# TensorE's turning of the first product's values ends after 12 jobs instead of 16 in the second MoE of a fused kernel

## The chip, the cores and the metric

The kernel runs on one core of a Trainium2 chip as one program. The core has five engines that run side by side, each its own list of instructions in order: TensorE (PE; the loading of its stationary operand is listed apart as PEld), VectorE (DVE), ScalarE (ACT), GpSimd (POOL) and SyncE (SP, which here only issues DMA transfers). An instruction waits on semaphores for what it needs, and everything behind it on the same engine waits with it. The metric is the device time of one execution in microseconds; the median of three runs is given, and the profile is one further execution of the same program.

## What is computed

Three parts follow one another: a chunked scan with decay ("attention"), a feed-forward layer h * cos(h) on its output, and a mixture of experts with one expert a token, 8 experts and a capacity. The change lies in the third part:

```python
def _moe2_ref(x, w_gate, w1, w2, capacity):      # x: 3072 x 256, w1: 8 x 256 x 1024, w2: 8 x 1024 x 256
    logits = x @ w_gate
    expert_idx = np.argmax(logits, axis=1)
    ...                                          # disp: each expert's tokens, in order, up to capacity
    h = np.maximum(np.einsum('ecd,edf->ecf', disp, w1), 0.0)
    y = np.einsum('ecf,efd->ecd', h, w2)
    out = np.zeros((N, D), dtype=np.float32)
    for i in range(N):
        if keep[i]:
            out[i] = gate_w[i] * y[expert_idx[i], pos[i]]
    return out.astype(np.float32)
```

## The kernel before, in words

**Blocks and jobs.** The tokens are sorted by expert into blocks of 128 tokens; each block belongs to one expert. 29 blocks are always computed. A job is a block and one half of the inner dimension (512 of 1024). Jobs 0 to 15 are the first halves of blocks 0 to 15; then come blocks 16 to 28 with both halves one after the other (job 16 is block 16's first half, job 17 its second, 18 and 19 are block 17's, 20 and 21 block 18's, and so on); last come the second halves of blocks 0 to 15. While the first 16 jobs run, other engines still prepare the weights of the second half (`w1b`, `w2b`), from transfers on SP at L1223.

**The steps of a job**, in the names of the code. `b_gather` (POOL, L1535) fetches a block's rows into `xr`, and `b_xt` (SP, L1552) turns them by a transposing transfer into `xk` (blocks 0 to 15 keep theirs in `xkeep`, since it serves two jobs far apart). `b_mm1` (TensorE, L1603) makes the first product in 6 matmuls into `hp`, in PSUM. `b_relu` (ScalarE, L1609) writes its positive part as f16 into the first half of `hr`; `b_low` (VectorE, L1613) writes what f16 has rounded off into the second half. Then `hr` (128 tokens by 2 x 512 values) has to be turned into `ht`, eight blocks of 128 x 128, so that the inner dimension lies on partitions. There are two ways for that in `b_turn`: for jobs below `NPT`, TensorE does eight transposes into PSUM (`tp`, L1630) and `b_tev` copies them to `ht` on ScalarE (L1639); for all others one transposing transfer on SP's queue writes `ht` from `hr` (L1634). `b_mm2` (TensorE, L1650) makes the second product in 12 matmuls into `yp`; `b_out` scales it by `sc` and writes or adds it to `yacc` (ScalarE at L1662 for first halves, VectorE at L1664 for second halves); `b_scat` (POOL, L1669) writes a finished block's rows to the output.

**Buffers.** `hr` takes a buffer of tag `g`, which has 6; `ht` takes one of the same 6, save for every fourth job, whose `ht` takes one of the 3 of tag `gl`, which the `xk` of blocks 16 and on use too. So a new `hr` or `ht` waits until the last reader of the old tile in its buffer is done: a turn on TensorE or a transfer on SP for an `hr`, the second product for an `ht`.

**What sets the order.** Every step is put on a list with a number from the table `PLACE`, by its kind and count (`'b1'` first product, `'br'` ReLU, `'bl'` low part, `'bt'` turn and, for jobs below `NPT`, its copy, `'b2'` second product, `'bx'` the transfer of `xk`, and so on). The list is sorted by these numbers, and each engine gets its instructions in that order. Before, the turns of jobs 12 to 15 have the places 1697, 1720, 1725 and 1749, their copies 1721, 1727, 1739 and 1754, and their second products 1740, 1744, 1760 and 1772.

## Time and profile before

| | us |
|---|---|
| three runs | 573.99, 568.50, 570.76 |
| median | 570.76 |
| the profiled execution, its own time | 568.56 |
| its span in the profile | 566.8 |

| busy, us (share of the span) | |
|---|---|
| TensorE, matmuls | 528.7 (93%) |
| VectorE | 415.7 (73%) |
| ScalarE | 379.2 (67%) |
| GpSimd | 355.6 (63%) |

Times in the trace count from the start of the span. The profile is read at four depths: the page's head and its busy shares; the busy time of each engine in a stretch, with the granted clock of TensorE and the busy share of the DMA engines; the chain of waits, followed back from the last instruction to what released each step; and single instructions in order of time, SP's queue among them. Arrows point from what is read to what is written: `ht<-hr` writes `ht` from `hr`.

## The change

`NPT` becomes 12, so jobs 12 to 15 take the second way of `b_turn`, the transposing transfer on SP; their copies by `b_tev` go, and with them their four numbers in the list `'bt'`. The four places 1697, 1720, 1725 and 1749, at which TensorE turned, are now those at which SP issues the transfers. No other number changes. The table is one line shorter, so each line of the changed kernel's code has a number that is lower by one (L1634 is L1633 there).

```diff
     'bt': [1533, 1534, 1562, 1593, 1587, 1588, 1594, 1596, 1605, 1617, 1622, 1628, 1636, 1644,
-        1653, 1655, 1661, 1671, 1674, 1688, 1685, 1690, 1705, 1713, 1697, 1721, 1720, 1727,
-        1725, 1739, 1749, 1754, 1765, 1763, 1779, 1780, 1794, 1800, 1821, 1813, 1826, 1844,
...
+        1653, 1655, 1661, 1671, 1674, 1688, 1685, 1690, 1705, 1713, 1697, 1720, 1725, 1749,
+        1765, 1763, 1779, 1780, 1794, 1800, 1821, 1813, 1826, 1844, 1845, 1851, 1865, 1880,
...
-    NPT = MSPL
+    NPT = 12
```

SP's queue before, from the last weight transfers ahead of job 12's turn to the first transfers of `ht`. `xk_4826`, `xk_4909`, `xk_4964` and `xk_5065` are those of blocks 16, 17, 18 and 19, `xkeep2_4548` is block 15's; `ht_5023` is job 17's, `ht_5027` job 16's. In brackets stand the semaphores that an issue waits for: DMAHW and DMASW are landings of earlier transfers, by slot.

```order
L1223 DMA wst3_4681<-in_w2_dram 128x4x256 [waits DMAHW5_49,DVE_49]
L1552 DMA_TRANSPOSE xk_4826<-xr_4577 128x4x128 [waits DMASW7_49,PE_49]
L1552 DMA_TRANSPOSE xkeep2_4548<-xr_4757 128x4x128 [waits DMAHW6_49,DMASW0_49]
L1223 DMA wst3_4843<-in_w2_dram 128x4x256 [waits DMAHW7_49,DMAHW0_49,DVE_49]
L1223 DMA wst2_4844<-in_w2_dram 128x4x256 [waits DMAHW1_49,DVE_49]
L1552 DMA_TRANSPOSE xk_4909<-xr_4831 128x4x128 [waits DMASW1_49,PE_49]
L1552 DMA_TRANSPOSE xk_4964<-xr_4895 128x4x128 [waits DMASW2_49,DMAHW2_49,PE_49,Activation_49]
L1634 DMA_TRANSPOSE ht_5023<-hr_4916 128x8x128 [waits DMAHW3_49,DVE_49,PE_49]
L1634 DMA_TRANSPOSE ht_5027<-hr_4942 128x8x128 [waits DMAHW5_49,DMAHW4_49,DVE_49]
L1552 DMA_TRANSPOSE xk_5065<-xr_4902 128x4x128 [waits DMAHW1_49,DMASW3_49,PE_49]
```

The same queue now, first from the same weight transfer to the two issues ahead of block 17's `xk`. `ht_4779`, `ht_4847` and `ht_4870` are those of jobs 12, 13 and 14; `xk_4819` and `xk_4884` are those of blocks 16 and 17.

```order
L1222 DMA wst3_4681<-in_w2_dram 128x4x256 [waits DMAHW5_49,DVE_49]
L1633 DMA_TRANSPOSE ht_4779<-hr_4721 128x8x128 [waits DVE_49]
L1551 DMA_TRANSPOSE xk_4819<-xr_4577 128x4x128 [waits DMAHW6_49,DMASW7_49,PE_49]
L1551 DMA_TRANSPOSE xkeep2_4548<-xr_4757 128x4x128 [waits DMAHW7_49,DMASW0_49]
L1222 DMA wst3_4836<-in_w2_dram 128x4x256 [waits DMAHW0_49,DVE_49]
L1222 DMA wst2_4837<-in_w2_dram 128x4x256 [waits DMAHW1_49,DVE_49]
L1633 DMA_TRANSPOSE ht_4847<-hr_4797 128x8x128 [waits DMAHW2_49,DVE_49,PE_49]
L1633 DMA_TRANSPOSE ht_4870<-hr_4822 128x8x128 [waits DMAHW3_49,DVE_49,PE_49]
L1551 DMA_TRANSPOSE xk_4884<-xr_4824 128x4x128 [waits DMAHW4_49,DMASW1_49]
```

Job 12's transfer stands behind the weight transfer, ahead of block 16's `xk`; those of jobs 13 and 14 stand behind the last two weight transfers and ahead of block 17's `xk`.

The second piece of SP's order follows right behind it. `xk_4937` is block 18's and `xk_5029` block 19's; `ht_4940` is job 15's, `ht_4987` job 17's and `ht_4991` job 16's.

```order
L1551 DMA_TRANSPOSE xk_4937<-xr_4872 128x4x128 [waits DMAHW5_49,DMASW2_49,PE_49]
L1633 DMA_TRANSPOSE ht_4940<-hr_4887 128x8x128 [waits DMAHW6_49,DVE_49]
L1633 DMA_TRANSPOSE ht_4987<-hr_4891 128x8x128 [waits DMAHW7_49,DMAHW6_49,DVE_49]
L1633 DMA_TRANSPOSE ht_4991<-hr_4915 128x8x128 [waits DMAHW0_49,DVE_49]
L1551 DMA_TRANSPOSE xk_5029<-xr_4877 128x4x128 [waits DMAHW1_49,DMAHW4_49,DMASW3_49,PE_49]
```

Job 15's transfer stands between block 18's `xk` and job 17's transfer. Job 17's `ht_4987` lies in the buffer of `hr_4887`, from which job 15's transfer reads, and waits for that transfer's landing (slot DMAHW6); before, job 17's stood right behind block 18's `xk` and waited for a turn of TensorE instead.

ScalarE before, from job 14's ReLU (`hr_4829`) to job 15's (`hr_4912`). `ht_4833`, `ht_4863` and `ht_4897` are the copies for jobs 11, 12 and 13.

```order
L1609 ACTIVATE hr_4829<-hp2_4725 128x512
L1639 ACTIVATE ht_4833<-tp_4809 128x1024
L1662 ACTIVATE yacc1_4762<-yp2_4788,sc_4777 128x256
L1639 ACTIVATE ht_4863<-tp_4779 128x1024
L1639 ACTIVATE ht_4897<-tp_4854 128x1024
L1662 ACTIVATE yacc1_4762<-yp2_4873,sc_4835 128x256
L1231 ACTIVATE w2b_4579,wsc4_4842<-wst3_4843 128x4x256
L1231 ACTIVATE w2b_4579,wsc4_4842<-wst2_4844 128x4x256
L1609 ACTIVATE hr_4912<-hp2_4866 128x512
```

And now, from job 14's ReLU (`hr_4822`) to job 15's (`hr_4887`); `ht_4826` is job 11's copy.

```order
L1608 ACTIVATE hr_4822<-hp2_4725 128x512
L1638 ACTIVATE ht_4826<-tp_4802 128x1024
L1661 ACTIVATE yacc1_4762<-yp2_4781,sc_4777 128x256
L1661 ACTIVATE yacc1_4762<-yp2_4857,sc_4828 128x256
L1230 ACTIVATE w2b_4579,wsc4_4835<-wst3_4836 128x4x256
L1230 ACTIVATE w2b_4579,wsc4_4835<-wst2_4837 128x4x256
L1608 ACTIVATE hr_4887<-hp2_4850 128x512
```

Two copies are gone from between the outputs of jobs 10 and 11; the outputs' order and job 15's ReLU behind them stay.

## Rows read from the trace of the kernel before

**Rows 1.** The page's head.

```profile
span 566.8 us, 10500 instructions
```

**Rows 2.** Busy time of the engines by stretch; the first line names the columns.

```profile
core 0: us, PE busy (x) PEld busy (x) DVE busy (x) ACT busy (x) POOL busy (x), PEclk, DMA share, GB/s
416.40:418.60 2.20, 0.06 (x1) 0.00 (x0) 2.20 (x4) 2.08 (x4) 0.00 (x0) 1.00 0.50 75
418.60:421.20 2.60, 2.54 (x7) 0.86 (x7) 0.69 (x3) 0.94 (x3) 1.38 (x3) 0.52 0.41 89
...
445.00:455.00 10.00, 10.00 (x68) 6.49 (x67) 7.50 (x15) 4.52 (x8) 2.91 (x7) 1.00 0.95 148
```

**Rows 3.** The same view, TensorE alone: its busy time, clock, DMA share.

```profile
435.50:438.50 3.00, 3.00 (x25) 1.00 0.97 275
438.50:443.00 4.50, 4.50 (x42) 1.00 0.28 67
```

**Rows 4.** The chain of waits, 425 to 460: start, duration in us, what.

```profile
432.56 0.45 PE tp L1630 x8
...
436.25 0.45 PE tp L1630 x8
...
439.31 0.45 PE tp L1630 x8
...
442.36 1.31 PE yp L1650 x12
...
443.79 0.47 PE tp L1630 x8
...
450.74 2.62 PE yp L1650 x24
```

**Rows 5.** SP's queue in order of time: start, duration in us, transfer, count.

```profile
432.60 1.84 SPq L1223 DMA_DIRECT2D wst<-in_w_dram  x2
...
442.97 1.19 SPq L1552 DMA_TRANSPOSE xk<-xr  x1
...
445.05 2.62 SPq L1634 DMA_TRANSPOSE ht<-hr  x2
...
449.75 1.23 SPq L1634 DMA_TRANSPOSE ht<-hr  x1
```

**Rows 6.** Order of time, 428 to 456; in brackets the idle time and its releaser.

```profile
428.71 0.69 DVE L1613 SCALAR_TENSOR_TENSOR hr<-hp,hr 128x512 f16<-128x512 f32 x1
...
433.97 0.68 DVE L1613 SCALAR_TENSOR_TENSOR hr<-hp,hr 128x512 f16<-128x512 f32 x1
...
439.24 1.04 POOL L1535 DMA_INDIRECT xr<-xs_d,gat  x1 [0.16 <-POOL gall L1553]
439.40 0.47 ACT L1662 ACTIVATE yacc<-yp,sc 128x256 f32<-128x256 f32 x1 [1.33 <-PE yp L1650]
...
442.47 0.69 DVE L1613 SCALAR_TENSOR_TENSOR hr<-hp,hr 128x512 f16<-128x512 f32 x1 [3.47 <-ACT hr L1609]
...
448.37 0.60 ACT L1609 ACTIVATE hr<-hp 128x512 f16<-128x512 f32 x1 [1.09 <-DMA ht<-hr]
...
450.58 2.78 PE L1650 MATMUL yp<-w2a,ht 128*128 x24
...
454.15 1.08 ACT L1609 ACTIVATE hr<-hp 128x512 f16<-128x512 f32 x2 [0.27 <-DMA ht<-hr]
```

**Rows 7.** Groups by line: count, busy us, mean ns, idle before and releaser.

```profile
L1639 ACT ACTIVATE ht<-tp 128x1024 f16<-128x1024 f16 x16 | 16.1, 1029 | 1.0 <-PE tp L1630 0.9
```

**Rows 8.** The chain of waits, 495 to 520: a transfer on it.

```profile
509.67 3.21 DMA ht<-hr
```

**Rows 9.** Order of time, 505 to 520.

```profile
512.98 0.60 ACT L1609 ACTIVATE hr<-hp 128x512 f16<-128x512 f32 x1 [6.43 <-DMA ht<-hr]
...
513.99 1.89 PE L1650 MATMUL yp<-w2b,ht 128*128 x12 [1.63 <-ACT yacc L1662]
```

**Rows 10.** Order of time, 550 to 566: the last scatter but one.

```profile
558.92 0.97 POOL L1669 DMA_INDIRECT out_dram<-yacc,scat  x1 [1.73 <-DVE yacc L1664]
```

## What is expected of the change, and why

> **What bounds the kernel now.** I read the profile from the outside in. The page's head gives the span of the profiled execution, 566.8 us [rows 1]; its own time is 568.56, so 1.76 lie around the span. The three runs are 568.50, 570.76 and 573.99: the profiled execution lies 2.20 below their median, so I make the sum against 568.56 and carry the difference over to 570.76.

> Next, busy time by stretch. Jobs 12 to 15 are computed between 432.4 and 455.0, and there TensorE is busy 3.00 of 3.00 us, 4.50 of 4.50 [rows 3] and 10.00 of 10.00 [rows 2], all at a granted clock of 1.00, while in the last of these no other engine is full. The reader should also see the DMA share: 0.97 from 435.5 to 438.5, 0.28 from 438.5 to 443.0 [rows 3], 0.95 from 445.0 to 455.0 [rows 2]. Third, the chain of waits: from 432.56 to 450.74 + 2.62 = 453.36 it consists of TensorE alone, with the four turns that the change takes away among its pieces [rows 4]. So in this stretch whatever leaves TensorE moves everything behind it up, until something else is late. What that could be is read from the transfer queue on SP [rows 5] and from the neighbours in order of time [rows 6].

> **What is removed.** On TensorE, four turns of eight transposes: 0.45, 0.45, 0.45 and 0.47 us for jobs 12 to 15 [rows 4], together 1.82, all on the path. That is the most that can be gained; the least is nothing, where TensorE then waits for something that was not late before. On ScalarE, four copies out of PSUM at 1029 ns [rows 7], 4.1 us. They are not on the path: at 439.40 ScalarE has waited 1.33 us for a product of TensorE [rows 6], and the ReLUs of jobs 15 and 17 stand behind that wait. I cost their loss at nothing; those ReLUs can come up only with TensorE, by the two turns that stand ahead of that wait, 0.90 (432.56 and 436.25 [rows 4]).

> **What is added.** Four transposing transfers on SP, 2.62 us for two issues [rows 5], so 1.3 each and 5.2 in all. From issue to use a transfer took 3.21 us where the chain of waits went through one [rows 8]; 3.3 for the nearest one (issued 445.05 [rows 5], ScalarE released 448.37 [rows 6]); and 4.40 for the slowest near here (issued 449.75 [rows 5], ScalarE released 454.15 [rows 6]). It cannot land before its issue ends, so 1.3 is the lower bound. I take 3.21: two of the three rows lie there, and job 15's transfer will have as little around it.

> Job 12: its low part is done at 428.71 + 0.69 = 429.40 [rows 6], its product stands right behind the turn of 439.31 [rows 4], so at 439.76, less at most three turns, 1.35: not before 438.4. That leaves 9 us for a transfer of 3.21. Cost nothing; SP's queue behind it is put back by at most one issue, 1.3.

> Jobs 13 and 14: job 13's low part ends at 433.97 + 0.68 = 434.65 [rows 6] and job 14's is the next on VectorE, behind the two weight loads issued at 432.60 [rows 5]. Those keep the DMA engines busy until 438.5 [rows 3]; two transfers more bring me to 438.5 + 2 x 1.3 = 441.1, in a stretch where the share was 0.28. Job 13's lands at about 439.8; its product is the one of 442.36 [rows 4], which, less three turns, 1.35, comes to 441.0, so it is there in time. Job 14's product stands behind two first products more. Cost nothing; without that cover up to 1.3, which the next step would hide.

> Job 15 is the step that decides. Its low part ends at 442.47 + 0.69 = 443.16 [rows 6] before and some 0.8 earlier after the change, but its transfer stands on SP behind the xk of block 18 (jobs 20 and 21), which leaves SP at 442.97 + 1.19 = 444.16 [rows 5]. That xk waits for the gather issued at 439.24 [rows 6], which moves up by the one turn that stands ahead of what releases it, 0.45. So job 15's transfer is issued at 443.7 and has landed at 443.7 + 3.21 = 446.9. The next transfer, job 17's, now waits for that landing, because it is written into the buffer that job 15's values are read from (the second piece of SP's order in the section on the change). Before, it started at 445.05 [rows 5]; now at 446.9. Behind it on SP stands job 16's: issued at 448.2, landed at 451.4. TensorE wants it for the second of the two products of the row at 450.58 [rows 6], at 450.58 + 1.31 = 451.89 before (1.31 is one product in [rows 4]), and 1.82 earlier, at 450.07, after the change. It waits 1.3 us and starts at 451.4, 0.5 earlier than before. What stands behind on SP catches up: the next transfer but one is issued at 450.7 where it was issued at 449.75, lands at 453.9, and releases the ReLU that started at 454.15. So of 1.82 gained, 1.3 is given back. After the one wait of this size that the trace has, 1.63, twelve matmuls took 1.89 us [rows 9], where 24 in one run took 2.78 [rows 6], 1.39 for twelve: 0.5 lost. I take off 0.2, less than half of it, as the wait here is shorter. **Sum: 1.82 - 1.3 - 0.2 = 0.3 us gained.**

> From job 18 on the order and the waits on SP are those of before, one place for one; TensorE is busy there all the time but for that one wait, and the last scatter but one still waits 1.73 us for VectorE's sum behind TensorE's last products [rows 10]. So I let the 0.3 go through to the end.

> [...] Here eight blocks of 128 x 128 cost TensorE 0.45 us on its path [rows 4] and a transfer of eight blocks 3.21 us until it can be used [rows 8]. [...]

> **The rivals.** All three follow from the same sum with another latency L from issue to landing: job 16's transfer lands at 443.7 + 1.3 + 2L. (B) All 1.82 stay: it lands by 450.07, which needs L of 2.53 or less. For it: TensorE has no other wait here, and 2.53 lies above the bound of 1.3. Against it: all three latencies above. 570.76 - 1.82 = 568.94. (C) Slower, by the same queue: it lands after 451.89, from L = 3.45 on. At 4.40 job 15's lands at 448.1, job 16's is issued at 449.4 and lands at 453.8, 1.9 behind the product of before. [...] For it: the DMA share of 0.95 right there; against it: one latency of three is over 3.45. (D) The end is paced elsewhere and the change moves nothing, 570.76: at 512.98 ScalarE had waited 6.43 us for a transfer, and TensorE for ScalarE [rows 9]. Against it: that run of transfers is itself started by TensorE's products.

> **How the numbers follow.** My forecast (a gain from 0 to 1.0, likeliest 0.3) has 0.45; B 0.20; C 0.20; D 0.15. Likeliest for the profiled execution 568.56 - 0.3 = 568.3, for the median 570.76 - 0.3 = 570.5. The range runs from the lowest run with all gained, 568.50 - 1.82 = 566.7, to C, 574.0, which is also the highest run with nothing gained. 1% is 5.7 us, about what a measurement of this kernel can tell from no change. No case reaches it; runs of one kernel lie 5.5 apart, so I leave 0.03 for faster and 0.05 for slower.

> **What would show it.** Right: the turns on TensorE and ScalarE's copies fall from 16 to 12, transfers of ht rise from 42 to 46; on SP a gap of about 2 us between the transfers of jobs 15 and 17; TensorE idle for about a microsecond before a product near 450, released by the DMA of ht; its products after 455 about 0.3 earlier than before. Wrong: no wait of TensorE between 445 and 455 (B), a wait over 2 us or a granted clock below 1.00 after it (C), or a new wait ahead of 445, for jobs 13 or 14 or for the xk behind them.

## The result, and the profile after

The change makes the kernel slower: 574.40 us (median of 7 runs, 572.75 to 577.07) against 570.60 for the kernel before (7 runs on the same chip), a ratio of 1.0067 with a 95% interval of 1.0041 to 1.0093. Forecast were 570.5 and a small gain; the time lies just above the range, which ended at 574.0. It is within 1%, which had 0.92, but it is a loss of 3.8 us where the sum said 0.3 gained.

The page of the changed kernel: head and busy times, then ScalarE's copies among the groups by line. Its profiled execution took 577.07 us, the longest of the 7; that of before took 568.56, next to its shortest. So the two spans differ by 8.5 us where the medians differ by 3.8, and the amounts read from the two traces below are larger than the median's loss.

```profile
span 575.3 us, 10438 instructions
PE 529.9 (92%) x3156; PEld 385.9 (67%) x3156; DVE 416.2 (72%) x877; ACT 375.7 (65%) x687; POOL 357.4 (62%) x422
...
L1638 ACT ACTIVATE ht<-tp 128x1024 f16<-128x1024 f16 x12 | 12.1, 1029 | 0.8 <-PE tp L1629 0.7
```

The work that was to go has gone: 12 copies where there were 16 [rows 7], 32 matmuls and 32 weight loads less on TensorE. But TensorE, which had no idle time between 432 and 455 [rows 2 to 4], now waits. In order of time on TensorE (start, duration, tile, count; in brackets the idle time ahead and what ended it):

```profile
436.72 1.46 PE L1602 MATMUL hp<-w1a,xkeep 128*128 x6 [0.26 <-DMA xkeep<-xr]
...
440.80 1.46 PE L1602 MATMUL hp<-w1a,xk 128*128 x6
...
446.12 2.72 PE L1602 MATMUL hp<-w1b,xk 128*128 x6 [2.04 <-DMA xk<-xr]
448.63 1.80 PE L1602 MATMUL hp<-w1a,xk 128*128 x6
450.27 1.47 PE L1649 MATMUL yp<-w2a,ht 128*128 x12
...
454.17 2.78 PE L1649 MATMUL yp<-w2a,ht 128*128 x24
```

The last line answers to the row at 450.58 [rows 6]: the second products of jobs 15 and 16 start 3.6 us later, although four turns of 1.82 us in all stand ahead of them no more. So between 432 and 454 some 5.4 us were lost: 3.6, and the 1.82 that the turns would have given. The largest piece is the wait of 2.04 for block 17's `xk`, the operand of job 18. The next is the slow stretch behind it (busy time by stretch, columns as in [rows 2]):

```profile
444.00:446.10 2.10, 0.08 (x1) 0.07 (x1) 1.22 (x5) 0.75 (x2) 0.00 (x0) 0.95 0.59 72
446.10:450.20 4.10, 4.08 (x12) 1.59 (x13) 2.19 (x8) 1.54 (x3) 3.27 (x6) 0.61 0.68 128
```

Over the 4.1 us behind the 2.04 us idle TensorE's granted clock is 0.61 on average, 0.50 from 446.1 to 449.0: its 12 matmuls (two first products) fill these 4.1 us, where the next two first products, from 451.58 to 454.17 in the same trace, took 2.59 at a clock of 1.00. That is 1.5 more. The rest, 1.9, went in small waits, most of them ahead of 440.8. Where the `xk` was is read on SP's queue (start, duration of the issue, count):

```profile
429.48 2.13 SPq L1633 DMA_TRANSPOSE ht<-hr  x1
431.71 1.20 SPq L1551 DMA_TRANSPOSE xk<-xr  x1
433.01 1.22 SPq L1551 DMA_TRANSPOSE xkeep<-xr  x1
434.32 1.09 SPq L1222 DMA_DIRECT2D wst<-in_w_dram  x2
435.51 5.23 SPq L1633 DMA_TRANSPOSE ht<-hr  x2
440.83 4.02 SPq L1551 DMA_TRANSPOSE xk<-xr  x2
444.94 5.76 SPq L1633 DMA_TRANSPOSE ht<-hr  x3
```

And the same queue before, at the two places that moved:

```profile
427.39 2.03 SPq L1552 DMA_TRANSPOSE xk<-xr  x1
...
436.68 7.48 SPq L1552 DMA_TRANSPOSE xk<-xr  x2
```

Job 12's transfer stands at the head of the queue and waits there for its own values. VectorE makes their low part until 428.77 + 0.68 = 429.45:

```profile
428.77 0.68 DVE L1612 SCALAR_TENSOR_TENSOR hr<-hp,hr 128x512 f16<-128x512 f32 x1
```

The transfer's issue then takes 2.13 us, so block 16's `xk` is issued at 431.71 instead of 427.39, half of that by the wait and half by the issue, and the last weights follow at 434.32 instead of 432.60 [rows 5]. Behind the weights the issues of jobs 13 and 14 take 5.23 us together, where two took 2.62 [rows 5], and block 17's `xk` leaves at 440.83 instead of 436.68.

The queue is not all of the 2.04, though. This is the DMA view from 442.5 to 446.5, 0.1 us to a digit (busy share in tenths; below, what moved in GB/s, and the packets of the instruction queue: count, MB, share):

```profile
DMA  0335699877999991300020099904999950003499
GB/s 0 41 85 165 131 270 313 267 254 172 280 215 202 156 80 36 41 0 0 0 44 0 0 44 28 56 18 100 279 289 289 267 24 0 0 0 38 90 233 195
...
q8 instruction: 1, 0.02, 1.5%
```

From 444.0 to 445.2, while block 17's `xk` is under way, nearly nothing moves: 56 GB/s at most, and 279 again from 445.3. The one packet of the instruction queue starts at 443.2. The experiments come back to such pauses; without this one, of some 1.2 us, the wait would have been about 0.8 (an estimate, the difference of the two).

## The experiments

Theories, as the expectations name them. **Q**: the loss comes from the order on SP's queue ahead of 446, new transfers that wait at its head or that keep others waiting. **R**: it comes from the one wait that the prediction singled out, job 17's transfer for the landing of job 15's. After the first four runs both had shown themselves, and **W** takes their place: the loss is all the new waits on SP's queue together, and nothing else. Its rival from there on is **F**: TensorE's fetches of its own instructions fall on other transfers, since 64 instructions are gone. A fetch is here a packet of the instruction queue on the page (30 packets and 0.49 MB in the kernel before, so 16 KB each); that these packets are TensorE's is F's assumption, and the last section has what the runs show of it.

### The parts alone

In each of the first three kernels only some jobs take the transfer; `b_turn` and the list of steps ask for membership, and `'bt'` keeps the copies' places of the others.

```diff
-    NPT = MSPL
+    TURN = [j for j in range(MSPL) if j not in (12,)]      # (13, 14) and (15,) in the other two
...
-        if j < NPT:
+        if j in TURN:
```

Job 12 alone:

> Only job 12's values are turned by a transfer (place 1697); TensorE turns those of the 15 other jobs. Theory Q (the loss comes from SP's queue ahead of 446: job 12's transfer stands first in it and waits for its values, block 16's xk and the last weights go out later behind it, jobs 13 and 14's transfers then stand ahead of block 17's xk, and TensorE waits 2.0 us for that xk at 446 and runs slowly after it): block 16's xk is issued at about 431.7 instead of 427.4 and the last weights about 1.7 later, TensorE waits 0.2 to 0.6 for them in all, but block 17's xk is issued by 438 and there is no wait of over 1 us at 446: 570.6 - 0.45 + 0.4 = 570.6, between 569.8 and 571.5. Theory R (the loss comes from job 17's transfer waiting for the landing of job 15's, as the prediction had it): that wait isn't in this kernel; 570.6 - 0.45 = 570.1.

Measured: 569.13 against 567.75 on the same chip, a ratio of 1.0029 [1.0007, 1.0051]. TensorE, at the place where Q said 0.2 to 0.6:

```profile
437.20 1.46 PE L1603 MATMUL hp<-w1a,xkeep 128*128 x6 [1.55 <-DMA xkeep<-xr]
```

The wait came, larger: 1.55 us for block 15's `xkeep`, which stands two places behind job 12's transfer. There is no wait at 446. The ratio lies above the range of Q, whose upper end was 571.5 of 570.6, 1.0016, though its interval reaches into it. Job 12 alone is a loss, and R can't explain it.

Jobs 13 and 14 alone:

> Only jobs 13 and 14 take the transfer. Theory Q: the last weights are issued at 432.6 and 434.1 as before, the two transfers stand behind them and land at about 440 to 442, block 17's xk is issued about 2 us later than before (438.5 to 439) and lands at 442.5 to 444, where TensorE wants it at 444.09 - 0.9 = 443.2: a wait of at most 1 us, smaller than the 2.04 of the changed kernel; 570.6 - 0.9 + 0.5 = 570.2, between 569.5 and 572. Theory R: no wait of job 17's transfer for a landing; 570.6 - 0.9 = 569.7.

Measured: 571.26 against 567.75, 1.0069 [1.0044, 1.0094]. TensorE waits 0.70 for block 17's `xk`, as Q had it:

```profile
446.54 1.46 PE L1603 MATMUL hp<-w1b,xk 128*128 x6 [0.70 <-DMA xk<-xr]
```

But the time is more than that wait and lies outside what Q allowed. In the trace (an execution of 574.56 us, the longest of the six) the rest appears step by step behind 453, at transfers whose order the kernel does not change. That was the first sign that something else was at work.

Job 15 alone:

> Only job 15 takes the transfer, so job 17's transfer waits for the landing of job 15's, and the queue ahead of it is that of before. Theory Q: block 17's xk goes out at 436.7 as before, TensorE loses nothing ahead of 446; job 15's transfer is issued at about 444.2, job 17's at 447.3 and job 16's at 448.6, landed at 451.8; TensorE wants it at 451.89 - 0.47 = 451.42 and waits at most 0.5: 570.6 - 0.47 + 0.4 = 570.5, between 569.8 and 571.2. Theory R: the whole loss of the change, 3.8 us, shows here: 574.4.

Measured: 571.46 against 567.75, 1.0065 [1.0039, 1.0091]: as much as the whole change, as R said, and outside the range of Q. But the three parts together make 1.6%, over twice the whole change, so they do not add up, and none of them by itself is the loss. TensorE and then three DMA issues (the last number is the time from issue to landing), those of job 15 (444.82), 17 (448.16) and 16 (449.49):

```profile
450.36 1.47 PE L1650 MATMUL yp<-w2a,ht 128*128 x12
454.29 1.83 PE L1650 MATMUL yp<-w2a,ht 128*128 x12 [2.46 <-DMA ht<-hr]
```

```profile
ht<-hr SPq DMA_TRANSPOSE x1, 3.3
```

```profile
ht<-hr SPq DMA_TRANSPOSE x1, 3.5
```

```profile
ht<-hr SPq DMA_TRANSPOSE x1, 4.7
```

So the mechanism of the prediction is there: job 17's transfer starts only when job 15's has landed, job 16's stands behind it, and TensorE waits. The size is not: 2.46 us where at most 0.5 was expected, because job 16's transfer took 4.7 us instead of 3.2. The DMA view of that stretch, 0.1 us to a digit (busy share in tenths; below, what moved), shows why:

```profile
DMA  9999999999999990000000001001799999999999
GB/s 223 207 233 197 179 213 374 193 215 212 218 197 143 42 11 0 0 10 5 10 10 8 10 10 18 3 0 26 120 200 200 215 212 200 218 223 210 182 174 187
...
q8 instruction: 1, 0.02, 1.7%
```

(451.5 to 455.5.) For 1.3 us nearly nothing moves, with three transposing transfers under way. The pause follows one packet of the instruction queue, 16 KB, which starts at 452.2. The trace of the kernel before has the same picture at 450 to 454, on the transfer for which the prediction had read 4.40 us:

```profile
DMA  9999200093999999990000000000008999999999
...
q8 instruction: 1, 0.02, 2.3%
```

There the packet starts at 450.8, nearly nothing moves from 451.8 to 453.0, 10 GB/s at most, and TensorE waits for none of the transfers under way (ScalarE waits 0.27 for one [rows 6]). So the 4.40 of [rows 5, 6] has a pause of 1.2 us in it; without it 3.2 would be left (an estimate, the difference of the two), next to the 3.21 and 3.3 that the prediction read elsewhere.

### Block 17's `xk` first, and a full reordering

```diff
-        1668, 1717, 1710, 1734, 1748, ...
+        1668, 1717, 1710, 1719, 1748, ...
```

> The changed kernel with one number moved: block 17's xk (place 1734) gets 1719, ahead of the transfers of jobs 13 and 14. Theory Q: it is issued at about 436.7, as soon as its gather has landed, and lands by 441; the wait of 2.04 us at 446 and the slow stretch behind it go, while jobs 13 and 14's transfers, 1.3 to 2.5 later, make TensorE wait up to 2 us for job 13's at about 441: 574.4 - 3.5 + 1.5 = 572.4, between 570.0 and 573.0, in any case below the changed kernel. Theory R: nothing changes at the wait of job 17's transfer; 574.4.

Measured: 572.98 against 567.75, 1.0106 [1.0070, 1.0143]. Q had it below the changed kernel in any case, and it is not: 1.0106 against 1.0067, with intervals that overlap. R, which had it equal, is not excluded by the time. The wait at 446 is gone, as Q said, but TensorE waits elsewhere:

```profile
434.90 1.46 PE L1602 MATMUL hp<-w1a,xkeep 128*128 x6 [0.68 <-DMA xkeep<-xr]
451.72 1.76 PE L1649 MATMUL yp<-w2a,ht 128*128 x12 [1.34 <-DMA ht<-hr]
```

The second line is the wait of R, 1.34 us, the size that the prediction gave it. In the changed kernel it was hidden: TensorE was already 3.6 us late there. From 431 to 453 this kernel lost 1.7 us against the kernel before (each measured from its own position at 431); more than half of the rest came between 510 and 517, far behind the transfers that were moved.

The full reordering moves three numbers of the changed kernel:

```diff
-        ... 1705, 1713, 1697, 1720, 1725, 1749, 1765, 1763, ...
+        ... 1705, 1713, 1717, 1720, 1725, 1749, 1765, 1766, ...
-        1668, 1717, 1710, 1734, 1748, ...
+        1668, 1717, 1710, 1719, 1748, ...
```

> The changed kernel with three numbers moved: job 12's transfer behind block 15's xk (1697 becomes 1717), block 17's xk ahead of jobs 13 and 14's transfers (1734 becomes 1719), and job 17's transfer behind job 16's (1763 becomes 1766). Theory W (the loss of the change is three waits that its order on SP's queue makes: job 12's values at the head of the queue, block 17's xk behind two transfers, job 16's transfer behind the wait for job 15's landing): TensorE's waits of 0.7 at 435, 2.0 at 446 and 1.3 to 2.5 at 452 go; what may stay is a wait of up to 1 us for job 13's transfer at 441. A ratio of 0.997 to 1.001 to the kernel before. Theory F (TensorE's fetches of instructions fall on other transfers): the ratio stays at 1.005 or above, with waits of TensorE for transfers in other places.

Measured: 578.10 against 568.94, 1.0163 [1.0125, 1.0200], the slowest of all, where W had 1.001 at most. W's order works for the other places, and by 441 the three turns are gained. But job 13's transfer, behind the last weights and block 17's `xk`, comes 3.1 us late, and TensorE's granted clock is 0.77 from 443 to 448, where it was 1.00 from 435 to 443:

```profile
444.18 2.00 PE L1649 MATMUL yp<-w2a,ht 128*128 x12 [3.10 <-DMA ht<-hr]
```

Part of the 3.1 us may again be a pause: a packet of the instruction queue starts at 440.5, while that transfer is under way. In the kernel with block 17's `xk` first, where the same transfers follow the weights in the same order, the product of job 13 shows no such wait; there TensorE came later to it, held up by block 15's `xkeep`. So job 13's transfer has little or no slack between the weights and its use; that it has none in any order is not shown.

### The wait for job 15's landing taken away

Job 15 alone again, with job 16's transfer ahead of job 17's (place 1763 becomes 1766). Job 17's `ht` then comes into another buffer and has no landing to wait for.

> Only job 15 takes the transfer, and job 16's transfer is issued ahead of job 17's (job 17's place 1763 becomes 1766), so it no longer stands behind the wait for job 15's landing. Theory W (in the kernel with job 15 alone the loss was TensorE's wait of 2.46 us for job 16's transfer, which came from that wait): job 16's transfer is issued at about 446.2 instead of 449.5 and lands by 450; TensorE has no wait before the second product of job 16, and the time falls from 571.5 to 567.75 - 0.47 = 567.3, between 566.5 and 568.5 on the chip where the kernel before has 567.75 (a ratio of 0.998 to 1.001). Theory F (the loss came from TensorE's own fetches of instructions, 16 KB each about 12 us apart, which fall on other transfers when the program has fewer instructions on TensorE; the trace shows transfers of 3.2 us stretched to 4.2 to 4.7 where such a fetch falls among them): 16 instructions fewer are 16 fewer in this order too, and the ratio stays at 1.004 or above.

Measured: 570.64 against 568.94, 1.0026 [1.0005, 1.0048], between the ranges of W (to 1.001) and F (from 1.004). TensorE has no wait for job 16's transfer; of the loss of 0.65% some 0.4 goes with that one place. What is left is not at that place (here TensorE, 3 us further on, with a packet of the instruction queue at 452.8):

```profile
455.16 1.46 PE L1603 MATMUL hp<-w1a,xk 128*128 x6 [0.99 <-DMA xk<-xr]
```

### The phase of the instruction fetches

By the phase this section means the instructions of the program at which the fetches fall. The kernel before, with inert matmuls where TensorE waits 4.93 us for VectorE at 398. They write a tile that the next instruction overwrites.

```diff
         pi = d['pi'] = pbank([P, 2, 20], "pi")
+        for _ in range(32 if part else 0):                  # 64, 96 and 128 in other kernels
+            nc.tensor.matmul(pi[:, 0, 0:n], id16, id16[:, 0:n], start=True, stop=True,
+                             skip_group_check=True)
```

> The kernel before with 32 matmuls of 19 columns added on TensorE, into a tile that is overwritten right after, where TensorE waits 4.93 us at 398 for VectorE; nothing else changes. They make 64 instructions, so TensorE's fetches of instructions come about 3 us earlier against the rest of the program from there on. Theory W (only the order on SP's queue matters): no change, a ratio of 0.999 to 1.001. Theory F: the number of fetches that fall among transposing transfers after 420, 4 of 12 in the trace of before, changes, and the time moves with it by 0.5 to 3 us, in most phases up: a ratio of 1.001 to 1.006.

Measured: 573.86 against 568.94, 1.0094 [1.0067, 1.0121]: 5 us lost by 64 instructions that do nothing and that lie in idle time. W, which had no change, falls as the only cause; F had the direction, and 1.006 at most:

```profile
397.13 0.95 PE L1130 MATMUL pi<-ncum 128*128 128x19 f16 x32
402.14 0.79 PE L1133 MATMUL pi<-ob,p_all 128*128 128x19 f16 x24 [4.07 <-DVE ob L1120]
```

> The kernel before with 128 of the inert matmuls at 398 instead of the 32 that made it 0.9% slower; at 0.03 us each they take 3.8 of the 4.93 us that TensorE waits there. They are 256 instructions with their weight loads, and the trace has a fetch of TensorE's instructions every 243 to 297 recorded ones, about 250 on average: a whole period. Theory F (what counts is at which instruction of the program a fetch falls): the fetches fall where they fell before, and the time returns to that of before, a ratio of 0.998 to 1.002. Rival P (the inert matmuls cost something by themselves, in TensorE's time or its clock): four times the matmuls cost more than 0.9%, a ratio of 1.009 or above.

Measured: 567.19 against 567.70, 1.0000 [0.9979, 1.0020]. (Over the whole trace of the kernel before the fetches lie 214 to 297 recorded TensorE instructions apart, 256 on average, but for the last one, 74 behind the one ahead of it.) Four times the matmuls cost nothing: what counts is not their work but at which instruction a fetch falls, and a whole period brings the time back. Rival P falls.

> The kernel before with 64 of the inert matmuls at 398 (128 instructions, half a period of the fetches). Theory F: a phase of its own, anywhere from 0.998 to 1.010. Theory W: 1.000, as the queue is that of before. With the ratios at 0, 32 and 96 matmuls (1.000, 1.0094, 1.0049) it gives the mean of the kernel before over four phases: 1.003 to 1.006.

Measured: 568.53 against 568.30, 1.0002 [0.9984, 1.0021]. By itself this decides nothing: both theories allowed it.

> The kernel before with 96 of the inert matmuls, 192 instructions: with a period of about 256 that is 64 instructions less than a whole one, which is what the change takes from TensorE. So from job 15 on the fetches fall at the same instructions as in the changed kernel, while all turns and SP's queue are those of before. Theory F: part of the change's loss shows here without the change, at 495 to 520 above all, where the changed kernel lost 4 us in its profiled execution: a ratio of 1.002 to 1.007. Theory W (only the order on SP's queue matters): 1.000.

Measured: 570.35 against 567.70, 1.0049 [1.0020, 1.0078]. Counted in instructions, 192 more than before and so 64 short of 256, this kernel has about the changed kernel's phase behind job 15, and not one of its transfers. Much of the time in these kernels goes at a place far from the change, the run of transfers at 513 that [rows 9] show. TensorE's wait there, with 32, 64, 96 and 128 matmuls (before: 1.63):

```profile
516.36 2.29 PE L1653 MATMUL yp<-w2b,ht 128*128 x12 [1.97 <-ACT yacc L1665]
```

```profile
514.67 1.78 PE L1653 MATMUL yp<-w2b,ht 128*128 x12 [1.77 <-ACT yacc L1665]
```

```profile
516.30 2.72 PE L1653 MATMUL yp<-w2b,ht 128*128 x12 [3.02 <-ACT yacc L1665]
```

```profile
513.12 1.86 PE L1653 MATMUL yp<-w2b,ht 128*128 x12 [1.35 <-ACT yacc L1665]
```

The order of the waits is not quite that of the times (32 has smaller waits at 500 besides, 0.38 and 0.39; the granted clock from 495 to 522 is 0.94 with 32 and with 96, 1.00 with 64 and 128), but the two slow kernels have the two long ones. Between 510 and 517 TensorE falls 1.8 us further behind the kernel before with 32 matmuls, 2.4 with 96 and at most 0.1 with 64 and 128. It is not the number of pauses that decides: behind 365 the trace with 128 has 8 fetches that go with one (counted as in the last section), as has that of the changed kernel. What fits the traces is that a pause costs time where it falls on a transfer for which something waits.

The same in the changed kernel:

> The changed kernel with the same 32 matmuls at 398, which give TensorE back the 64 instructions that the change took away, so that from job 15 on a fetch falls at the same instruction as in the kernel before. Theory W: the wait of 2.0 us at 446 and the slow stretch behind it stay, a ratio of 1.005 to 1.008. Theory F: the fetch that stretched block 17's xk at 443.2 falls 3 us earlier, the wait at 446 shrinks below 1.2 us, and of the losses behind 460 (4.2 us in the profiled execution of the changed kernel) most go: a ratio of 1.000 to 1.004.

Measured: 576.43 against 568.94, 1.0135 [1.0107, 1.0163]. F expected that the phase of before would take the loss away, and it was doubled; W, with 1.008 at most, missed too. The trace is of an execution of 572.98 us, the shortest of the six. In it the wait at 446 is gone and behind 460 only 0.6 us are lost, as F had it, but now TensorE waits for job 13's transfer, with a fetch at 437.5, and 13 us later for job 16's, with the next at 451.1:

```profile
439.97 2.41 PE L1652 MATMUL yp<-w2a,ht 128*128 x12 [1.96 <-DMA ht<-hr]
453.51 2.17 PE L1652 MATMUL yp<-w2a,ht 128*128 x12 [2.26 <-DMA ht<-hr]
```

So F alone falls too: a phase that is harmless for the kernel before is not harmless here, as other transfers are late.

> The changed kernel with 64 of the inert matmuls. Theory W and F together: the waits on SP's queue come in each phase, on top of what the phase costs; with the ratios at 0 and 32 matmuls (1.0067, 1.0135) and that at 96 the mean over four phases is 0.4 to 0.8% above that of the kernel before: a ratio of 1.006 to 1.014 here. Theory F alone (the change only moved the phase): both means are alike, and this one lies at 1.000 to 1.004.

Measured: 573.49 against 568.30, 1.0092 [1.0059, 1.0124]: W and F together. TensorE waits 1.99 us for job 13's transfer, 0.35 for block 17's `xk` and, as the prediction had it, for job 16's transfer:

```profile
454.35 1.87 PE L1652 MATMUL yp<-w2a,ht 128*128 x12 [1.61 <-DMA ht<-hr]
```

> The changed kernel with 96 of the inert matmuls, a whole period less two times the 64 instructions: W and F together: 1.006 to 1.014; F alone: 1.000 to 1.004.

Measured: 571.78 against 568.30, 1.0072 [1.0046, 1.0097]: W and F together again. Job 16's transfer:

```profile
453.40 1.76 PE L1652 MATMUL yp<-w2a,ht 128*128 x12 [1.90 <-DMA ht<-hr]
```

Together, ratios to the kernel before by the number of inert matmuls:

| | 0 | 32 | 64 | 96 | mean |
|---|---|---|---|---|---|
| kernel before | 1 | 1.0094 | 1.0002 | 1.0049 | 1.0036 |
| changed kernel | 1.0067 | 1.0135 | 1.0092 | 1.0072 | 1.0092 |

Over these four phases the change costs 0.55% on average, 3.1 us. The noise of the runs makes that uncertain by some 0.2%; but the four differences lie between 0.23 and 0.90%, so other phases could give another mean. The phase alone moves either kernel, by up to 0.9% and 0.7%. The kernel before stands in one of its good phases.

That the change costs something in every phase is shown better by place. How much later TensorE's second products come than in the trace of the kernel before, in us, counted from each trace's own position at 431 and split at 460 (one execution each; a gain of turns is already in it):

| inert matmuls | 0 | 32 | 64 | 96 |
|---|---|---|---|---|
| kernel before, 431 to 460 | 0 | 0.0 | 0.0 | 0.0 |
| changed kernel, 431 to 460 | 3.5 | 6.4 | 3.5 | 2.5 |
| kernel before, behind 460 | 0 | 3.9 | 0.7 | 1.8 |
| changed kernel, behind 460 | 4.1 | 0.6 | 3.3 | 1.8 |

Where the transfers are new, no phase of the kernel before loses anything and each phase of the changed kernel does: that is W, with the waits in other places and sizes from phase to phase, as pauses fall on these transfers or do not. Behind 460, where the order is that of before, both kernels lose by the phase: that is F.

### Versions that keep a gain

> Job 15 alone by transfer, job 16's transfer ahead of job 17's, and 8 of the inert matmuls at 398, which replace the 16 instructions of the turn that is gone, so that behind job 15 the fetches fall at the same instructions as before. Theories W and F together: neither the wait for job 16's transfer nor new collisions are left, and the turn's 0.47 us stays gained: a ratio of 0.997 to 1.001. Theory F wrong: as without the 8 matmuls, 1.0026.

Measured: 567.93 against 567.70, 1.0001 [0.9982, 1.0020]. With the wait for job 15's landing gone and the instructions given back, the loss of 0.65% is gone as W and F together have it. The last step, from 1.0026 without the 8 matmuls, is within the noise by itself: the two intervals overlap. In the traces the wait of 0.99 for an `xk` at 455 is gone with it. Of the 0.47 us that a turn takes nothing can be seen in the time; in the trace TensorE gains 0.4 on its own position at 431, until it waits 0.35 for VectorE at 456.9.

> Jobs 12, 14 and 15 by transfer, job 13 by TensorE: job 12's transfer behind block 15's xk (1717), job 14's behind block 17's xk (1734), job 17's behind job 16's (1766), and 24 inert matmuls at 398 for the three turns that are gone. No transfer of a block's xk stands behind one of ht that waits, and job 13, whose transfer came too late, has none. Theories W and F together: 3 x 0.45 = 1.35 us gained, if the transfers themselves keep nothing waiting: a ratio of 0.996 to 1.000. Where a transfer still comes too late (job 12's is issued only at 432.5 and wanted at 438): a wait of 1 to 2 us and 1.000 to 1.004.

Measured: 569.10 against 567.70, 1.0016 [0.9992, 1.0039]. Up to 451 TensorE has no wait and the three turns are gained (1.2 of 1.35 us). Then:

```profile
455.04 1.46 PE L1606 MATMUL hp<-w1a,xk 128*128 x6 [1.59 <-DMA xk<-xr]
```

> Jobs 12, 14 and 15 by transfer in the order of the last such kernel, with 12 inert matmuls instead of 24. There TensorE was 1.25 us ahead of its start by 451, and then waited 1.59 us for block 19's xk, which took 5.7 us instead of 3.2, a fetch at 453.12 falling between its packets. With 24 instructions less the fetch comes about 1.1 us later, behind that xk's landing. Theory F: the wait goes and the gain stays, a ratio of 0.996 to 1.000. Where the wait came from the queue: it stays, 1.0016.

Measured: 570.63 against 568.30, 1.0043 [1.0021, 1.0066]; a miss. The wait for that `xk` is gone, but TensorE waits 1.15 for VectorE's low part instead, and more is lost behind. The fetch did not come 1.1 us later: it starts 2.9 us behind the start of job 15's second product in both kernels (at 453.1 and 450.26 there, at 451.4 and 448.46 here), and falls on the next transfers. No version that was run is faster than the kernel before.

## Why the prediction was wrong, by its steps

**What is removed** was right as far as the runs show it: three turns gave 1.2 to 1.3 us of their 1.35 where nothing else was late yet (the full reordering up to 441, three transfers with 24 matmuls up to 451). That ScalarE's copies were worth nothing no run shows by itself; nothing speaks against it.

**Job 12** failed. "SP's queue behind it is put back by at most one issue, 1.3" counted the issue and forgot that the transfer waits at the head of the queue for its own values: the low part was done at 429.4, and block 16's `xk` had gone out at 427.4. It was put back by 4.3 us, 2.1 of waiting and 2.2 for an issue that took 2.13 instead of 1.3. The step looked at whether the transfer would be in time for its user, and it was; who stood behind it in the queue was not looked at. Alone it cost 0.29%.

**Jobs 13 and 14** failed. The sum put their transfers behind the weights, landed at 439.8 and 441.1, which supposes that the queue ahead stays where it was and that a transfer starts moving as soon as the weights leave. The weights came 1.7 later by the step before, the two issues took 5.23 instead of 2.6, and block 17's `xk`, which stands behind them, came 2.04 too late, with a pause of 1.2 in its own transfer; the slow clock behind that wait took 1.5 more. In two other phases it was job 13's transfer that came too late, by 1.96 and 1.99, where the step said that it is there in time. The prediction named both among what would prove it wrong ("for jobs 13 or 14 or for the xk behind them") and gave the wait for the `xk` no price. The order of the queue, shown in the section on the change, had it.

**Job 15** was right in its mechanism and wrong in its size. The wait for the landing, the gap on SP and the late transfer of job 16 came, 1.34 us with block 17's `xk` out of the way against 1.3 in the sum. That agreement is partly luck: counted from the position at 431, both TensorE and the transfer came some 1.8 us later there than the sum had them. It was 2.46 where a fetch fell on that transfer, so the latency L, 3.21 in the sum, was 4.7 there. No transfer came near the lower bound of 1.3, the end of the issue: with job 15 alone two issues took 2.62 from 448.16, and their transfers landed 3.5 and 4.7 us after each began; in the trace of the kernel before the packets of each of the 71 transposing transfers, counted off in the queue's order, end behind its issue. In the changed kernel itself the wait did not show, because TensorE came 3.6 us late for other reasons; in its three other phases it did, with 2.26, 1.61 and 1.90. Rival C, slower by the same queue at L = 4.40, gave 574.0, within 0.4 of the median, but that was luck: it came by another place than the one that lost the time. Its 574.0 is 570.76 + 1.9 + 1.3, the 1.3 an estimate from 2.6 us at a granted clock of 0.52 behind 2.2 us of waiting [rows 2]. That term was right in size: 1.5 was measured after 2.04, over 4.1 us at 0.61.

**"From job 18 on the order and the waits on SP are those of before"** holds for the order and not for the time. With 64 instructions less on TensorE the fetches come at other places (430.2, 443.2 and 457.6 in the changed kernel's trace, 427.6, 439.4 and 450.8 in that of before), and in the profiled execution TensorE lost another 4.1 us behind 460. The sum put this at nothing, because the order there does not change. How much of the median's loss that is in this one phase can't be said from these runs: the 0.55% is a mean over phases, and a phase that was good for the kernel before was bad for this one. The kernel before in about the changed kernel's phase (96 matmuls) was at 1.0049, the changed kernel at 1.0067.

A transfer of eight blocks took 3.3 to 4.7 us with job 15 alone, and TensorE's turn of eight 0.45 to 0.47 [rows 4]; what the transfers cost lay in the queue around them.

## What to carry to other kernels

A step moved onto a queue has two prices: whether it is in time for its own user, and what it does to each transfer behind it, from the moment when it reaches the head of the queue and waits for its input; look up both for every entry behind it, row by row (here block 16's `xk` went out 4.3 us later behind job 12's transfer). Where transfers have little slack, read whether a long latency in the trace has a pause of the DMA engines in it (here 1.2 of 4.40 us) before taking it for the queue's own, and look whether a change in TensorE's number of instructions has moved such pauses (64 less on TensorE, and the packet of 439.4 came at 443.2 here). A difference of half a per cent between two versions of such a kernel is not a verdict on the idea until both have been timed in several phases of the fetch, which some inert instructions in idle time give (128 of them cost nothing here).

## What the runs showed of the hardware that was not expected

```profile
q8 instruction: 30, 0.49, 0.4%
```

```profile
q8 instruction: 31, 0.51, 0.4%
```

  The 256 instructions brought the time back to 1.0000, where 64 had cost 0.94%. The place of a fetch against the products is not exact, though: with as many instructions as before, or a whole period more, the one near 451 starts 0.2 us behind the start of job 15's second product in the kernel before, 0.5 with 128 matmuls, 1.4 with job 15 alone swapped and 8, and 2.9 with three transfers and 24.
- In the DMA views above, nearly nothing moves for 1.2 us from 451.8 (kernel before), 1.2 from 444.0 (changed kernel) and 1.3 from 453.0 (job 15 alone), each time 0.8 to 1.0 us behind the start of such a packet and with transposing transfers under way. With job 15 alone the transfer with that pause in it landed 4.7 us after its issue began, the two ahead of it 3.3 and 3.5. Counted from the traces of all 18 kernels: of 117 times behind 365 us at which five or more transposing packets took over 0.9 us, 108 go with such a fetch. The other way round, 106 of the 272 fetches there go with such a pause. The connexion is one of time in all traces; what in the chip makes the engines stand still no run shows.
- Two transposing issues that followed two transfers of 512 KB of weights took 5.23 us on SP in the changed kernel (from 435.51) and 4.54 with jobs 13 and 14 alone (from 437.19), where two took 2.62 in the kernel before [rows 5].
- After 2.04 us idle TensorE's granted clock in the changed kernel was 0.61 over the next 4.1 us, 0.50 up to 449.0, and 1.00 from 450.2 on.
